# One constant to the front of GpSimd's stream, and a later start for the first filter and table loads, in a spectral-mixing and MLP kernel

## The chip, the cores and the metric

One core of one Trainium2 chip. The metric is the device time of one execution in microseconds, as a median of several executions. The record sorts executions into a fast and a slow state (slow: over 1.5% above the fastest of the same kernel). Profiles are of one execution; "us" positions in them count from the start of its span. A single execution scatters by about 1 us around the median.

## The reference, cut to what matters

```python
def _layernorm(x, axis=-1, eps=1e-5): ...

def reference(A_x, A_w_r, A_w_i, B_x, B_w1, B_b1, B_w2):
    # A: rfft2 over both axes, times a complex filter w_r + i w_i, irfft2
    # B: einsum with w1, + b1, mish, einsum with w2
    x = A_x                                     # (1, 2048, 1024) bf16
    x = x + A(_layernorm(x), A_w_r, A_w_i)
    x = x + B(_layernorm(x), B_w1, B_b1, B_w2)
    x = x + A(_layernorm(x), A_w_r, A_w_i)
    x = x + B(_layernorm(x), B_w1, B_b1, B_w2)
    return x
```

The Fourier transforms are done as matrix products. Only the first layernorm and the start of the first A are touched by the change.

## The kernel before

The kernel builds five instruction streams: PE (TensorE, the matrix products), DVE (VectorE), ACT (ScalarE), POOL (GpSimd) and SP (SyncE, which only issues transfers here). `self.op(engine, fn, reads=, writes=)` appends to an engine's stream and works out what it must wait for from the named resources; `self.dma(engine, ...)` does so for a transfer that this engine issues. An engine executes its stream in order. The opening issues these loads:

```python
    def prologue(self):
        sp = self.sp
        xt = self.x[0].rearrange("(t p) d -> p t d", p=P)
        for c in range(4):                       # x by rows: 16 row tiles, 4 quarters of 1 MB
            self.dma(sp, self.XS[:, 4*c:4*c+4, :], xt[:, 4*c:4*c+4, :], f"x{c}", writes=self.r_xs[4*c:4*c+4])
        # ... M0, IDF
        for q in range(4):                       # XR: x transposed for the first product, 32 pieces of 128 KB
            r = Res(f"xr{q}")
            for h in range(8):
                prog = self.pool if q and h % 2 else sp
                self.dma(prog, self.XR.ap[h:P:8, 32*q:32*q+32, :], xv[h][:, 32*q:32*q+32, :], f"xr{q}{prog.name}",
                         parts=[r], reads=[self.r_xs[15]] if prog is self.pool else [])
            self.r_xr.append(r)
            if q == 2:
                self.dma(sp, self.FD[:], self.con["FD"], "fd", writes=[self.r_fd])
        # ... JT
        self.op(self.pool, lambda e: e.memset(self.EPS[:], 1e-5), writes=[self.r_eps, self.r_warm])
        self.warm(ACT.Sqrt)                      # ACT: one sqrt of EPS, so that its table is loaded early
```

`reads=[self.r_xs[15]]` on a load is a gate: the load doesn't need x, it is only held back until the last rows of x are in memory. The statistics of the 16 row tiles are then split between DVE and ACT:

```python
    def first_scales(self):
        for j in range(0, 16, 4):
            n = 2 if j % 8 else 3
            for i in range(n):
                self.stats_dve(j + i)            # bn_stats, 10 tiles in all
            for i in range(n, 4):
                self.stats_act(j + i)            # Copy and Square with accumulation, 6 tiles
            self.sums_to_mv(j + n, 4 - n)        # 3 small DVE ops: ACT's sums to mean and variance
        self.root(0, 16)                         # ACT sqrt, DVE reciprocal
        # ... PE transpose of the scales
```

After that, in `s1`, DVE and ACT scale 128 copies of a small matrix M (four groups of eight ahead of their use), PE multiplies them with XR in 16 groups of eight, and DVE and ACT copy the results out of PSUM, the memory that PE writes. Groups 0 to 3 need XR's first quarter, 4 to 7 its second, and so on. The next product stage, with FD, is called s2; the first inverse product comes later in the same A. Then the filters of `load_wr` and the tables are used:

```python
    def load_wr(self, wr, g):
        # ... for the real and the imaginary part:
            self.dma(self.pool, wr.ap[:, c, :, :], rows, "l" + wr.res.name, parts=[wr.res],
                     reads=[self.r_xs[15]] if g < 2 else [])
```

## Time and profile before

| | before |
|---|---|
| time, median | 1065.87 us (3 runs) |
| PE busy | 90% of the span |
| first PE instruction | 38.9 us |
| scaling of M starts | 39.85 us |

The chain of waits, followed back from the last instruction, in order of time (start us, us, what), is read as "this is what the end of the kernel waited for". Its first pieces and the first scaling:

```profile
2.34 11.88 DMA XS<-in_A_x_dram
14.51 7.61 POOL ARENA L249 x12
22.49 1.05 ACT ARENA L440 x2
...
39.85 3.34 DVE ARENA L573 x20
```

Load of x, then twelve DMA issues of POOL, then ACT's statistics, then DVE. L249 is the line of the helper that issues a DMA, L440 ACT's statistics, L573 the scaling of M.

### The profile page before, as it was taken

How to read it: one execution, taken by the hardware profiler on the slowest of the kernel's cores; microseconds unless marked ns; L12 is line 12 of the kernel's file. 1: busy time of each engine (PE TensorE's matmuls, PEld its weight loads, DVE VectorE, ACT ScalarE, POOL GpSimd, SP SyncE). 2: the span in 40 equal slices, each digit the busy share in tenths (PEclk: the TensorE clock that was granted, in tenths of full speed). 3: DMA queues.
4: the chain of work that ended last, by engine and by line, in shares of the span. 5: the costliest groups of instructions: out<-in, count | busy, mean ns of one | idle time of the engine just before them, and what ended most of it. 6: DMA issues, size and time to landing. Idle time of an engine off the chain costs nothing.

```text
span 1065.6 us, 14183 instructions
## 1 busy us (share of the span) xinstructions
PE 959.8 (90%) x6033; PEld 513.0 (48%) x6033; DVE 352.0 (33%) x776; ACT 336.5 (32%) x503; POOL 71.0 (7%) x114
## 2 busy tenths in 40 slices
PE   0389768999999999999977985899999999999998
PEld 0267556444444444444435764754444444444443
DVE  2879755260343200023434775526011100000111
ACT  2888635333000143410006963533400014341000
POOL 4024000000000000000530200000000000000000
PEclk9999969999999999999998995999999999999999
DMA  9639860456111122000751677045611122200000
GB/s 278 159 94 310 229 170 13 151 173 207 46 55 45 44 79 60 1 10 20 191 103 23 210 202 186 1 145 191 199 45 35 54 66 73 66 1 10 21 20 30
DMA packets 152718, 107.01 MB, mean 100 GB/s; under 512 B 74288, under 2 KB 131888, under 8 KB 152656
## 3 DMA queue, kind: packets, MB, share of 16 engines
q1 hardware_dynamic: 139936, 75.99, 24.9%
q0 software_dynamic: 9632, 28.45, 9.1%
q10 hardware_dynamic: 3088, 1.67, 0.6%
q8 instruction: 48, 0.79, 0.3%
q14 instruction: 14, 0.11, 0.0%
HBM read 80.85 MB, written 20.71 MB: 95 GB/s over the span
## 4 chain that ended last, share of the span: by engine, by line
PE 79%; DVE 9%; ACT 6%; DMA 3%; issue 1%; POOL 1%; SPq 0%; ACTq 0%; DVEq 0%
PE PS L976 36%; PE PS L994 36%; PE PS L669 2%; ACT ARENA L721 2%; DVE XS L915 1%; DVE ARENA L573 1%; DMA XS<-in_A_x_dram 1%; DVE ARENA L790 1%; DVE BN L459 1%; ACT ARENA L440 1%; DMA u_scratch<-ARENA 1%; DMA ARENA<-u_scratch 1%; DVE ARENA L951 1%; DVE ARENA L596 1%; PE PS L901 1%
## 5 line engine op out<-in xcount | busy, mean ns | idle before, releaser
L976 PE MATMUL PS<-ARENA 128*128 128x512 bf16 (+1 forms) x1984 | 394.8, 361 | 8.3 <-DVE ARENA L951 7.2
L994 PE MATMUL PS<-ARENA 128*128 128x512 bf16 x1792 | 387.4, 379 | 0.0
L980 ACT ACTIVATE ARENA<-PS,B 128x512 bf16<-128x512 f32 (+1 forms) x248 | 159.8, 646 | 439.4 <-PE PS L976 439.4
L976 PEld LDWEIGHTS PS<-ARENA 128*128 128x128 bf16 x1984 | 194.4, 99 | 202.2 <-DVE ARENA L951 8.7
L994 PEld LDWEIGHTS PS<-ARENA 128*128 128x128 bf16 x1792 | 175.3, 98 | 211.4
L999 DVE TENSOR_TENSOR XS<-PS,XS 128x512 bf16<-128x512 f32 x64 | 44.3, 692 | 537.4 <-PE PS L994 537.4
L459 DVE BATCH_NORM_STATS2 BN<-XS 128x6 f32<-128x512 bf16 x104 | 67.1, 675 | 7.4 <-DMA XS<-in_A_x_dram 6.2
L915 DVE TENSOR_TENSOR XS<-PS,XS 128x512 bf16<-128x512 f32 (+1 forms) x40 | 29.1, 790 | 82.1 <-PE PS L901 82.1
L901 PE MATMUL PS<-MT,ARENA 128*128 128x32 bf16 (+1 forms) x768 | 24.7, 188 | 27.2 <-DMA ARENA<-u_scratch 24.0
L901 PEld LDWEIGHTS PS<-MT,ARENA 128*128 128x128 bf16 x768 | 23.3, 101 | 30.8 <-issue 24.3
L669 PE MATMUL PS<-FD,ARENA 128*128 128x256 bf16 (+1 forms) x256 | 34.5, 283 | 2.9 <-ACT ARENA L594 1.2
L721 ACT ACTIVATE ARENA<-PS 128x1024 bf16<-128x1024 f32 x32 | 33.8, 1058 | 8.5 <-PE PS L717 8.5
L554 PE MATMUL PS<-ARENA 128*128 128x128 f32 x1 | 0.5, 472 | 38.9 <-DVE ARENA L551 38.9
L440 ACT ACTIVATE ARENA<-XS 128x1024 bf16<-128x1024 bf16 x24 | 25.3, 1054 | 32.3 <-DVE XS L915 31.6
L750 ACT ACTIVATE ARENA<-PS 128x1024 bf16<-128x1024 f32 x32 | 33.9, 1059 | 3.7 <-PE PS L743 3.7
L249 POOL DMA_DIRECT2D xn_scratch<-ARENA x15 | 8.3, 551 | 391.1 <-DVE ARENA L498 391.1
L743 PE MATMUL PS<-ARENA 128*128 128x256 bf16 x256 | 33.2, 273 | 0.1
L431 ACT ACTIVATE RS<-MV,EPS 128x1 f32<-128x1 f32 (+1 forms) x7 | 2.0, 292 | 98.4 <-DVE MV L462 96.2
L725 DVE TENSOR_TENSOR ARENA<-ARENA 128x1024 bf16<-128x1024 bf16 x32 | 22.0, 688 | 22.7 <-ACT ARENA L721 22.7
L743 PEld LDWEIGHTS PS<-ARENA 128*128 128x128 bf16 x256 | 24.5, 98 | 10.0 <-DVE ARENA L732 1.2
L669 PEld LDWEIGHTS PS<-FD,ARENA 128*128 128x128 bf16 x256 | 25.1, 102 | 8.7 <-DVE ARENA L596 2.8
L764 PE MATMUL PS<-ARENA,BD 128*128 128x256 bf16 x192 | 25.9, 273 | 1.3 <-DVE ARENA L790 1.0
(70 smaller groups left out, 535.7 us busy)
## 6 DMA issues: line engine op xcount, KB each, us to landing
ARENA<-in_B_w_dram SPq DMA_DIRECT2D x56, 512.0 KB, 3.9
ARENA<-in_B_w_dram SPq DMA_DIRECT2D x56, 256.0 KB, 4.4
u_scratch<-ARENA SPq DMA_DIRECT2D x14, 512.0 KB, 3.4
ARENA<-u_scratch SPq DMA_DIRECT2D x14, 512.0 KB, 5.6
XS<-in_A_x_dram SPq DMA_DIRECT2D x4, 1024.0 KB, 8.7
w_scratch<-ARENA POOLq DMA_DIRECT2D x8, 512.0 KB, 5.4
ARENA<-w_scratch POOLq DMA_DIRECT2D x8, 512.0 KB, 5.1
out_dram<-XS SPq DMA_DIRECT2D x16, 256.0 KB, 2.2
```

The lines of the kernel that those rows point to most:

```text
L440: self.op(act, lambda e, i=i, f=f: e.activation(junk.ap, x, f, accum_out=sums[:, i:i + 1]), reads=[self.r_xs[j]], writes=[junk.res], parts ...
L459: self.op(self.dve, lambda e: e.bn_stats(self.BN[:, j, 6 * h:6 * h + 6], self.XS[:, j, 512 * h:512 * h + 512]), reads=[self.r_xs[j]], part ...
L669: fns.append(lambda e: e.matmul(dst, at(r), FD[:, t:t + n], start=start, stop=stop))
L721: self.op(act, lambda e: e.activation(x.ap.rearrange("p a b -> p (a b)"), ps, ACT.Copy, scale=SIG), reads=banks, writes=[x.res])
L743: fns.append(lambda e, c=c, part=part: e.matmul(ps[:, c * 256:(c + 1) * 256], yk.ap[:, part, c * P:(c + 1) * P], t[:, (128, 0)[part]:(384, ...
L750: self.op(act, lambda e: e.activation(v.ap[:, :, i, :], src, ACT.Copy), reads=banks, parts=[v.res])
L901: fns.append(lambda e, l=l: e.matmul(ps[:, w * l:w * l + w], self.UT.ap[:, u0 + l, :], self.MT[:, 8 * lo:8 * lo + w], start=True, stop=True))
L915: self.op(self.dve, lambda e: e.tensor_tensor(xs, src, xs, ALU.add), reads=rb, parts=self.r_xs[lo:lo + nb])
L976: fns.append(lambda e, db=db, bank=bank, fl=fl: e.matmul(PS[:, bank, 0:w], wb.ap[:, db, fl * P:(fl + 1) * P], x.ap[:, db, tok], start=(db ...
L980: self.op(act, lambda e, bank=bank, ft=ft: e.activation(at.ap[:, ft, tok], PS[:, bank, 0:w], ACT.Mish, bias=self.B1[:, ft:ft + 1]), reads= ...
L994: fns.append(lambda e, i=i, ft=ft: e.matmul(PS[:, bank, :], at.ap[:, ft, t * P:(t + 1) * P], W2[ft].ap[:, h * 512:(h + 1) * 512], start=(i ...
L999: self.op(dve, lambda e: e.tensor_tensor(xs, PS[:, bank, :], xs, ALU.add), reads=[self.r_bank[bank]], writes=[self.r_xs[j]])
```

## The change

Intent: let ACT's statistics start when x arrives, and keep the first filter and table loads off the DMA engines until all of XR is loaded.

```diff
     def prologue(self):
         sp = self.sp
+        self.op(self.pool, lambda e: e.memset(self.EPS[:], 1e-5), writes=[self.r_eps, self.r_warm])
+        self.warm(ACT.Sqrt)
         xt = self.x[0].rearrange("(t p) d -> p t d", p=P)
@@
         self.JT, self.r_jt = small["JT"].ap, small["JT"].res
-        self.op(self.pool, lambda e: e.memset(self.EPS[:], 1e-5), writes=[self.r_eps, self.r_warm])
-        self.warm(ACT.Sqrt)
         self.w1_next = 0
@@ def load_wr
-                     reads=[self.r_xs[15]] if g < 2 else [])
+                     reads=[self.r_xr[3]] if g < 2 else [])
```

## The prediction

> **What bounds the kernel now.** I read the page first (engine shares, chain, waits), then the timeline of the first 65 us, because both edits touch only instructions that run there, then the waits of that stretch, then the DMA view in short windows, and last the trace's landing records of single transfers. Over the whole span PE is 90% busy and carries 79% of the chain, but at the start it does nothing:
>
> ```profile
> PE PS L554 <- DVE ARENA L551: 38.9, 1, 38.9
> ACT EPS L424 <- POOL EPS L401: 20.3, 1, 20.3
> DVE MV L451 <- ACT ARENA L440: 15.5, 2, 14.2
> POOL ARENA L249 <- DMA XS<-in_A_x_dram: 14.1, 1, 14.1
> ```
>
> These are waits of the first 70 us: who waited for whom, us in total, times, longest. Read from the bottom they are one queue of dominoes. POOL (GpSimd) sits until the last rows of x land at 14.1; ACT waits 20.3 us for a constant that POOL writes; DVE waits 14.2 us for ACT's statistics; PE's first matmul comes at 38.9. The timeline shows why (start, us, what):
>
> ```profile
> 0.75 1.28 ACT L424 ACT_TABLE_LOAD   x1 [0.75 <-PEq L1168]
> ...
> 10.33 0.21 DVE L462 BATCH_NORM_AGGREGATE MV<-BN 128x2 f32<-128x12 f32 x1
> 14.51 7.61 POOL L249 DMA_DIRECT2D ARENA<-in_A_x_dram  x12 [14.06 <-DMA XS<-in_A_x_dram]
> 22.11 0.14 POOL L401 MEMSET EPS<- 128x32 f32 x1
> ...
> 22.29 0.20 ACT L424 ACTIVATE EPS<-EPS 128x1 f32<-128x1 f32 x1 [20.26 <-POOL EPS L401]
> 22.40 1.04 ACT L440 ACTIVATE ARENA<-XS 128x1024 bf16<-128x1024 bf16 x1
> ...
> 24.74 0.28 DVE L451 TENSOR_SCALAR MV<-BN 128x2 f32<-128x2 f32 x1 [14.21 <-ACT ARENA L440]
> ...
> 38.03 0.31 ACT L431 ACTIVATE RS<-MV,EPS 128x16 f32<-128x16 f32 x1 [1.39 <-DVE MV L453]
> ...
> 39.85 3.34 DVE L573 TENSOR_SCALAR ARENA<-ARENA 128x128 bf16<-128x128 bf16 x20
> ```
>
> The 0.14 us memset stands in POOL's stream behind twelve DMA issues (7.61 us) that themselves wait for x. The layernorm statistics of 16 row tiles are shared: DVE does ten (bn_stats), ACT six (two passes each). ACT starts at 22.40 though its first tile was in memory at 6.2, when DVE began.
>
> The other resource of this stretch is the DMA engines: busy at nearly 100% from 2 to 41 us. Two windows, 10-20 us and then 28-31 us, queue by queue (packets, MB, share of 16 engines):
>
> ```profile
> q1 hardware_dynamic: 5135, 2.46, 87.9%
> q0 software_dynamic: 167, 0.47, 19.6%
> ```
> ```profile
> q0 software_dynamic: 342, 1.12, 96.5%
> q1 hardware_dynamic: 154, 0.04, 5.8%
> ```
>
> q1 carries what SP issues (x by rows, then 20 of the 32 pieces of XR, the transposed view of x, in 256-byte rows); q0 carries what POOL issues (the other 12 pieces, then filter and table loads). At 28-31 us filters and tables take nearly everything and XR almost stops.
>
> **What the Trainium skill says.** "Trainium Architecture — The Big Picture", section "Inside one NeuronCore": engines have their own streams and synchronize only through semaphores. The trace agrees: one semaphore from a 0.14 us memset holds ACT for 20.3 us. "TensorE: Matmul & The Clock Gate", section "Architectural detail: the array is 16× 32×32, not 1× 128×128": ACT and DVE queues are strict FIFO, so ACT's ready statistics cannot pass its waiting warm-up. The trace agrees, nothing of ACT runs between 2.0 and 22.29. "DMA: Bandwidth & Descriptors", section "Issuing engines are not separate DMA queues": transfers of all issuers run on the same 16 engines and interleave. The windows above agree. "TensorE: Matmul & The Clock Gate", section "What's actually happening": the clock gate decides in free-running windows of 3413 ns. The recorded clock changes lie at 132.18, 145.83, 149.24, 156.07, which are multiples of 3.41 us apart; so a shift of the start is not passed on exactly to later stages.
>
> **The change, part by part.** Instruction counts do not change. On POOL one memset moves ahead of twelve DMA issues; the order on PE, DVE, ACT and SP is the same. The first four filter and first four table issues now wait for all of XR's last quarter instead of the last rows of x.
>
> Part 1, the memset. It runs at about 0.5 us; the warm-up follows the table load at about 2.1. Now ACT's six tiles follow the data. The four quarters of x land at 6.2, 9.0, 11.5, 14.2 (issue time plus time to landing). One tile on ACT costs 2 x (1.06 + 0.12 until the next pass) = 2.36 us. ACT: tile 3 from 6.2 to 8.6; tiles 6 and 7 from 9.0 to 13.7; tile 11 to 16.1; 14 and 15 to 20.8. DVE, by durations of before: three tiles 6.2 to 10.5; three small ops 0.54 to 11.1; two tiles 2.9 to 14.0; small ops 0.5 to 14.5; three tiles 4.2 to 18.7; small ops 0.55 to 19.25; two tiles 2.83 to 22.1; small ops 0.55 to 22.65. DVE never waits for ACT on this list, if narrowly (ACT 13.7 against DVE 14.0). Root, reciprocal, transpose and copy (38.03 to 39.85 before) take 1.8, so the scaling of M starts at 24.5 instead of 39.85: 15.35 us earlier. It cannot be the whole 20.3 us that ACT waited: 6.2 us of those are x still on its way, and DVE takes over as the bound.
>
> Part 2, the wait. The first product stage then starts at 24.5 and takes 22.2 us (39.85 to 62.05), bound by DVE. It needs XR quarter by quarter: the first at about 25.6, the second at 45.19 - 15.35 = 29.8, the third at 35.3, the fourth at 40.8. Before, the quarters were complete at 22.2, 33.9, 35.8 and 39.8 by the landing records. So without part 2 the second would come about 4 us late. With part 2, POOL's share of XR is still done by 28.5, and q1 has the engines to itself from about 27. My estimate: the second quarter's last three straggling pieces (29.9 to 33.9 before, all others by 27.1) come by 28; then 3.5 pieces left of the third at 0.25 MB/us (q1 alone did 0.48 MB in 14-16 us) end by 30, the FD table (0.65 MB at about 0.39) by 31.5, the fourth quarter's four pieces by 33 to 34. All three are in time, with 1.8, 5 and 7 us to spare.
>
> What the wait delays: filters and tables are issued from about 33.5, eight issues of 5.3 us (22.18 to 27.2 before), landing within 7 us: filter 0 by about 41, the last table by 46. The first user, the DVE copy at 61.92, moves to 46.6 and the first table's matmul from 67.9 to 52.5. At least 5 us to spare for the filter, so the new wait is hidden. JT and FD, which follow on q1, land earlier than before.
>
> Sum: 15.35 us (part 1) + 0 of cost (part 2, which protects about 4 us of it). Behind this stage each later one only shifts. 1065.87 - 15.4 = 1050.5 us, 1.4% less.
>
> **The rivals.** (a) The XR load takes the place of the memset: if q1 does not speed up, the second quarter lands near 34 and PE stalls 4 us: 1054.5. For it: the DMA engines are full until 41 us and 256-byte rows run at only 0.24 MB/us; against: what starved q1 was 1.8 MB of filters and tables, which are now gone. (b) The filters come too late: waiting for XR, then 5.3 us of issues, then landing; it would need them over 5 us later than I estimate. Each us more costs one: perhaps 1053-1056. Against it: little else is left on the queues by then. (c) ACT is slower or DVE waits for ACT: at most a us, as ACT has 1.3 us of slack at the end. (d) All 20.3 us come back: no, x's landing forbids it; the most that ACT's own start can give is 22.40 - 6.24 = 16.2. That is also why over 2% (21.3 us) is not within reach. (e) Nothing: if XR's arrival set the start. Against: in the trace of before no PE wait on XR is seen at all.
>
> **Range and chances.** The step of 15.35 is read from durations that vary by under 2%. Uncertain is a possible stall of 0 to 4 us on XR, and the clock windows, which may move one or two us either way over some six cold stretches; the three runs of before spread by 1.9. So 1050.5, and 8 in 10 within 1047.5 to 1054.5. Faster by over 2% (below 1044.6): 0.02. Slower by over 2%: 0.01. Within 2%: 0.97.
>
> **What would show it.** Right: POOL's memset before 1 us, ACT's first tile at 6.2, DVE without a wait over 1 us after 11 us, the scaling of M at 24 to 25, no PE wait on XR, the filter copy near 46.6, POOL's filter issues at 33-34. A PE or DVE wait on a DMA between 25 and 47 us shows (a) or (b). Wrong would be the sum if the stages after 47 us do not keep their lengths of before (78 us up to the first inverse product, 264.0 - 140.0 = 124 us after it).

## The result, and the profile after

The changed kernel took 1050.93 us (median of 4 runs, 1050.21 to 1051.88), against 1065.73 for the kernel before in the same rounds. The ratio is 0.9859, 95% interval 0.9842 to 0.9876, 15 us or 1.4% less. A ratio is the mean time of one kernel's fast runs over that of the other's of the same rounds, so it isn't quite the ratio of the medians.

The chain of waits of the changed kernel, first pieces:

```profile
0.74 5.50 DMA XS<-in_A_x_dram
6.27 1.30 DVE BN L459 x2
7.80 1.16 DVE BN L459 x2
...
20.34 1.16 DVE BN L459 x2
24.02 3.34 DVE ARENA L573 x20
```

POOL's issues and ACT's statistics are gone from it. The chain now waits only for the first quarter of x, and from 6.27 on it is nearly all DVE's own work; what is left out between 20.34 and 24.02 holds ACT's square root (0.32 us) and PE's transpose (0.49). The timeline around it (in brackets: idle before, and what ended it):

```profile
0.74 0.12 POOL L375 MEMSET EPS<- 128x32 f32 x1 [0.29 <-POOLq L1168]
...
2.04 0.20 ACT L424 ACTIVATE EPS<-EPS 128x1 f32<-128x1 f32 x1
...
6.27 1.06 ACT L440 ACTIVATE ARENA<-XS 128x1024 bf16<-128x1024 bf16 x1 [4.03 <-DMA XS<-in_A_x_dram]
...
22.20 0.31 ACT L431 ACTIVATE RS<-MV,EPS 128x16 f32<-128x16 f32 x1 [1.41 <-DVE MV L453]
...
34.65 0.73 POOL L249 DMA_DIRECT2D ARENA<-in_A_w_r_dram  x1 [12.61 <-DMA ARENA<-in_A_x_dram]
```

The constant is written at 0.74 instead of 22.11, ACT's first tile runs at 6.27 instead of 22.40, and the square root at 22.20 instead of 38.03. The last line is the new wait: POOL stands still for 12.61 us, until XR is complete, and then issues the filters at 34.65.

Where the time went, by landmarks of the two traces (us):

| | before | after | difference |
|---|---|---|---|
| scaling of M starts | 39.85 | 24.02 | -15.83 |
| first product to next stage (s2) | 21.08 | 21.10 | 0.0 |
| s2 to first inverse product | 77.94 | 76.89 | -1.05 |
| inverse product to second GEMM of B | 123.84 | 123.70 | -0.1 |
| from there to the second A's first product | 301.12 | 302.21 | +1.1 |
| first product to s2 in the second A | 11.49 | 12.25 | +0.8 |
| the rest (inverse product, B, end) | 489.16 | 488.28 | -0.9 |

The whole gain is made before the scaling starts. The other rows are of the size of the scatter between executions; the traces of the experiments show what two of them are (-1.05 and +0.8, see the last part of the experiments).

Landings of transfers, from the trace's landing records (us): XR's quarters were complete at 22.1, 33.9, 35.8, 39.8 before and at 21.4, 28.4, 30.5, 34.4 after; filter 0 at 29.9 before and 41.4 after.

### The profile page after: what moved, and what is told of

Read it like the earlier page. It is cut to its first block, busy times and chain, and to the rows that moved or that the text cites. A ratio compares the mean times of both kernels' runs of the same rounds, so it can differ in the third digit from the quotient of the medians.

```text
span 1049.6 us, 14096 instructions
## 1 busy us (share of the span) xinstructions
PE 952.5 (91%) x5944; PEld 511.7 (49%) x6033; DVE 350.8 (33%) x776; ACT 336.5 (32%) x503; POOL 71.0 (7%) x114
## 4 chain that ended last, share of the span: by engine, by line
PE 80%; DVE 9%; ACT 6%; DMA 3%; issue 1%; SPq 0%; ACTq 0%; DVEq 0%
PE PS L994 37%; PE PS L976 37%; DVE BN L459 2%; ACT ARENA L721 2%; PE PS L669 2%; DVE XS L915 1%; DVE ARENA L573 1%; DVE ARENA L790 1%; DMA u_scratch<-ARENA 1%; DMA ARENA<-u_scratch 1%; ACT ARENA L704 1%; DVE ARENA L951 1%; DVE ARENA L596 1%; PE PS L901 1%; ACT ARENA L792 1%
## 5 line engine op out<-in xcount | busy, mean ns | idle before, releaser
L976 PE MATMUL PS<-ARENA 128*128 128x512 bf16 (+1 forms) x1946 | 390.6, 360 | 10.3 <-DVE ARENA L951 7.2
L901 PE MATMUL PS<-MT,ARENA 128*128 128x32 bf16 (+1 forms) x768 | 24.5, 187 | 27.2 <-DMA ARENA<-u_scratch 23.8
L440 ACT ACTIVATE ARENA<-XS 128x1024 bf16<-128x1024 bf16 x24 | 25.3, 1055 | 36.4 <-DVE XS L915 31.5
L721 ACT ACTIVATE ARENA<-PS 128x1024 bf16<-128x1024 f32 x32 | 33.9, 1060 | 8.5 <-PE PS L717 8.5
L750 ACT ACTIVATE ARENA<-PS 128x1024 bf16<-128x1024 f32 x32 | 33.9, 1061 | 3.7 <-PE PS L743 3.7
L498 DVE TENSOR_SCALAR ARENA<-XS,MV,RS 128x1024 bf16<-128x1024 bf16 x48 | 25.0, 543 | 1.0
```

Of the source, the lines that this page charges most:

```text
L721: self.op(act, lambda e: e.activation(x.ap.rearrange("p a b -> p (a b)"), ps, ACT.Copy, scale=SIG), reads=banks, writes=[x.res])
L750: self.op(act, lambda e: e.activation(v.ap[:, :, i, :], src, ACT.Copy), reads=banks, parts=[v.res])
L901: fns.append(lambda e, l=l: e.matmul(ps[:, w * l:w * l + w], self.UT.ap[:, u0 + l, :], self.MT[:, 8 * lo:8 * lo + w], start=True, stop=True))
L976: fns.append(lambda e, db=db, bank=bank, fl=fl: e.matmul(PS[:, bank, 0:w], wb.ap[:, db, fl * P:(fl + 1) * P], x.ap[:, db, tok], start=(db ...
```

## The experiments

Kernels are compared only within the same rounds.

| run | median us | ratio to before, 95% | first product at | length of the product stage |
|---|---|---|---|---|
| r0_after_again | 1051.75 | 0.9855 (0.9842 to 0.9868) | 25.12 | 21.09 |
| e1_memset_only | 1051.05 | 0.9866 (0.9848 to 0.9884) | 25.23 | 21.09 |
| e2_wait_only | 1066.23 | 0.9992 (0.9980 to 1.0005) | 41.01 | 21.10 |
| e3_late_memset_free_warmup | 1050.59 | 0.9847 (0.9833 to 0.9860) | 25.12 | 21.09 |
| e4_memset_after_first_issue | 1060.51 | 0.9937 (0.9924 to 0.9949) | 34.03 | 21.09 |
| e5_filters_later | 1051.84 | 0.9858 (0.9845 to 0.9871) | 25.31 | 21.19 |
| e6_filters_after_second_quarter | 1050.32 | 0.9839 (0.9826 to 0.9853) | 25.32 | 21.09 |
| e7_one_conversion | 1049.73 | 0.9838 (0.9825 to 0.9852) | 24.41 | 21.11 |
| r1_after_third | 1050.53 | 0.9846 (0.9832 to 0.9861) | 25.21 | 21.12 |
| e1b_memset_only_repeat | 1051.33 | 0.9853 (0.9838 to 0.9867) | 25.43 | 21.09 |
| e7b_one_conversion_repeat | 1049.41 | 0.9837 (0.9822 to 0.9852) | 24.52 | 21.08 |
| e8_second_quarter_last | 1053.87 | 0.9875 (0.9859 to 0.9892) | 25.13 | 25.45 |

r0 to e3 ran on one chip, e4 to e7 on a second, the last four on a third. "First product" and "product stage" are read in the trace of one execution each.

**r0_after_again and r1_after_third**: no edit, the changed kernel again.

> The changed kernel once more, on the same chip as the next three. Both theories: 1050.9 us within 1 us, 14.8 us less than before. In the trace the scaling of M starts at 24.0 us. Stage lengths after that may differ by 1 to 2 us from the first trace, where the cold stretches of the tensor clock fall differently; if the landmarks of this trace repeat those of the first one exactly, that reading of the differences falls.

> The changed kernel a third time, for comparison on one chip with the next three: 1050 to 1052 us, a ratio of 0.9857 within 0.0015 to before; scaling of M at 24.0 us, 21.1 us from the first product to the next stage.

Measured: ratios 0.9855 and 0.9846. In r0 the stage after s2 took 78.05 us instead of 76.89, so the landmarks of the first trace did not repeat exactly, as expected. The three ratios of the changed kernel (with 0.9859) give the size of what can't be told apart here: about 0.001, or 1 us.

**e1_memset_only**: the memset first, the filters gated by x alone as before.

```diff
-                     reads=[self.r_xr[3]] if g < 2 else [])
+                     reads=[self.r_xs[15]] if g < 2 else [])
```

> Memset first, filters and tables wait for x alone as before. My theory: ACT and DVE as in the changed kernel (scaling at 24.0 us), but filters and tables take the DMA engines from 27 to 32 us and the second quarter of XR lands at about 34 as before, while its first matmul wants it at 29.4: a PE wait of about 4.5 us on a DMA, time 1055.4 us (1054 to 1057). The rival, that the second edit is idle and the memset does it all: 1050.9 us and no PE wait on a DMA.

Measured: 1051.05 us, the same as the changed kernel, with one of four runs at 1055.38. So the step of my theory that gave 4 us to the second edit failed. The landing records say that XR did come late: its second quarter at 30.3 and its third at 36.8, while in the changed kernel PE had started the groups that need them at 29.4 and 34.9. The timeline of this run shows why that was free (PE's product groups, DVE's copies out of PSUM and scalings):

```profile
34.00 1.72 DVE L573 TENSOR_SCALAR ARENA<-ARENA 128x128 bf16<-128x128 bf16 x10
35.62 1.22 DVE L596 CAST ARENA<-PS 128x1024 bf16<-128x1024 f32 x1
...
36.76 1.72 DVE L573 TENSOR_SCALAR ARENA<-ARENA 128x128 bf16<-128x128 bf16 x10
36.91 3.17 PE L588 MATMUL PS<-ARENA 128*128 128x128 bf16 x32 [2.72 <-DVE ARENA L596]
38.38 1.23 DVE L596 CAST ARENA<-PS 128x1024 bf16<-128x1024 f32 x1
```

PE waited 2.72 us and then did 32 matmuls in one go; DVE went on without a gap. The profile puts PE's wait down to DVE's copy, which ended at 36.84; XR's third quarter landed at 36.8, so here two releasers fall together. That it was XR is my reading, as PE had passed the same place at 34.88 in the changed kernel, with DVE at the same point of its work.

New theory: DVE is the bound of this stage, and PE leads it. Two lines of the changed kernel's timeline, group 4 on PE and its copy by DVE:

```profile
29.36 0.62 PE L588 MATMUL PS<-ARENA 128*128 128x128 bf16 x8 [0.57 <-DVE ARENA L573]
...
32.79 1.21 DVE L596 CAST ARENA<-PS 128x1024 bf16<-128x1024 f32 x1
```

PE starts the group at 29.36, and DVE copies it out at 32.79. The group took 0.62 us here, but groups done at PE's slower pace take about 1.0 (1.01 for the one at 33.09). Reckoned with 1.0, PE has 2.4 us of lead, and a late XR costs only what goes beyond a landing at 31.8.

**e1b_memset_only_repeat**: the same kernel again, for the scatter.

> The memset alone once more, because three of its four fast runs did as well as the changed kernel and one took 1055.38. My new reading: the second quarter of XR lands early or late by chance of its last pieces (30.3 in the traced run, 33.9 in the trace of before), and PE runs some 2.4 us ahead of the DVE copy that frees its banks, so that only a landing after about 31.8 costs. Then most runs lie at 1050 to 1052 and some few at 1053 to 1056; the median is within 1 us of the changed kernel. The rival, that 1055.38 was an accident that has nothing to do with the filters: all runs within 1052.5, as those of the changed kernel.

Measured: 1051.33 us, four runs from 1050.37 to 1052.68; XR's second quarter landed at 27.1 in the traced one. Eight runs without the wait have a mean of 1051.67, twelve runs with it (first result, r0, r1) 1051.02. The difference of 0.65 us comes from one run, 1055.38, and no trace was taken of that run. That its XR landed late is likely but not shown, and neither reading of this experiment is settled by it.

**e8_second_quarter_last**: the direct test of the lead. XR's quarters are issued in the order 1, 3, 4, 2, and the filters wait for the second.

```diff
-        for q in range(4):
-            r = Res(f"xr{q}")
+        # ... the four Res objects are now made before the loop
+        for k, q in enumerate((0, 2, 3, 1)):
+            r = self.r_xr[q]
@@
-                prog = self.pool if q and h % 2 else sp
+                prog = self.pool if k and h % 2 else sp
@@
-            if q == 2:
+            if k == 2:
@@ def load_wr
-                     reads=[self.r_xr[3]] if g < 2 else [])
+                     reads=[self.r_xr[1]] if g < 2 else [])
```

> The changed kernel with XR's second quarter issued last (order 1, 3, 4, 2; the filters wait for it, so they are issued as late as now): the same traffic, and the second quarter lands at 34.4 to 36.7, where the fourth did. The theory of the prediction, that every us after 29.4 costs one: 5.0 to 7.3 us more. The theory that a wait of PE costs only beyond the 2.4 us by which it leads DVE's copy (copy of the fifth group at 32.8, its eight matmuls take 1.0, so the harmless landing ends at 31.8): 2.6 to 4.9 us more, 1053.5 to 1056, and by the landing L in the trace itself, the stretch from the first product to the next stage is 21.1 + (L - 31.8). A third, that PE has more lead than that: less than 2 us more.

Measured: 1053.87 us, 3.3 more than the changed kernel on the same chip by the medians (ratios 0.9875 against 0.9846). The second quarter landed at 36.0. The timeline of this run:

```profile
31.15 1.71 DVE L572 TENSOR_SCALAR ARENA<-ARENA 128x128 bf16<-128x128 bf16 x10
36.08 4.58 PE L587 MATMUL PS<-ARENA 128*128 128x128 bf16 x48 [7.31 <-DMA ARENA<-in_A_x_dram]
37.13 1.22 DVE L595 CAST ARENA<-PS 128x1024 bf16<-128x1024 f32 x1 [4.28 <-PE PS L587]
```

PE waited 7.31 us on the DMA, but DVE waited only 4.28 us, and the stage grew by 25.45 - 21.10 = 4.35. The rule with 2.4 us of lead had said 21.1 + (36.0 - 31.8) = 25.3; the theory of the prediction, one us for each after 29.4, would have given 27.7. (The time grew by only 3.3 us in the medians; the landing is known for this one execution alone.) So the lead is shown: the wait of the engine that isn't the bound costs nothing until the bound itself waits.

**e2_wait_only**: the other edit alone, on the kernel before.

```diff
-                     reads=[self.r_xs[15]] if g < 2 else [])
+                     reads=[self.r_xr[3]] if g < 2 else [])
```

> Memset late as before, filters wait for all of XR. My theory: XR lands 4 to 6 us earlier than before (last quarter at 34 to 35 instead of 39.8) and nobody profits, because the start of the scaling is still set by ACT, at 39.85: 1065.7 us, within 1 us of before. The rival, that the traffic of filters and tables slowed the opening stage by itself: some us faster than before, 1060 to 1064.

Measured: 1066.23 us, ratio 0.9992, the same as before. XR's quarters landed at 20.9, 26.0, 30.6 and 34.5, over 5 us earlier than before for the last three, and the first product stayed at 41.01. Faster loads that nobody waits for gain nothing.

**e3_late_memset_free_warmup**: the constant late as before, but ACT's warm-up fed by DVE.

```diff
-        self.op(self.pool, lambda e: e.memset(self.EPS[:], 1e-5), writes=[self.r_eps, self.r_warm])
-        self.warm(ACT.Sqrt)
+        cell = Res("cell")
+        self.op(self.dve, lambda e: e.memset(self.RS[:, 3, 0:1], 1.0), writes=[cell])
+        self.op(self.act, lambda e: e.activation(self.RS[:, 3, 1:2], self.RS[:, 3, 0:1], ACT.Sqrt), reads=[cell])
@@ at the end of prologue
+        self.op(self.pool, lambda e: e.memset(self.EPS[:], 1e-5), writes=[self.r_eps, self.r_warm])
```

> The memset stays late in POOL's stream (at about 22.1 us) with the filters waiting for XR, but ACT's warm-up reads a cell that DVE writes at the start, so that nothing holds ACT's queue before the square root at about 22.2. My theory, that the loss came from a waiting instruction at the head of an in-order queue and not from the constant being late: ACT's first tile at 6.3 us, scaling at 24.0 to 24.3, 1050.9 us (1050 to 1052). The rival, that the constant itself has to be early: about 1065.7 us. A third outcome, a table load that is paid again before the square root: 1.3 us more, 1052.3.

Measured: 1050.59 us, as the changed kernel. Its timeline:

```profile
6.18 1.06 ACT L442 ACTIVATE ARENA<-XS 128x1024 bf16<-128x1024 bf16 x1 [3.94 <-DMA XS<-in_A_x_dram]
...
21.93 0.14 POOL L404 MEMSET EPS<- 128x32 f32 x1
22.17 0.31 ACT L433 ACTIVATE RS<-MV,EPS 128x16 f32<-128x16 f32 x1 [1.42 <-DVE MV L455]
```

The memset ran at 21.93, as late as before, and its real user at 22.17 didn't wait for it, if only by 0.1 us. (The two lines of 6 and 21 us are from two windows of the same timeline.) So the constant wasn't late. What cost 16 us was that an early, unimportant reader of it stood at the head of ACT's in-order stream.

**e4_memset_after_first_issue**: the memset behind one of POOL's twelve issues.

```diff
@@ at the head of prologue
-        self.op(self.pool, lambda e: e.memset(self.EPS[:], 1e-5), writes=[self.r_eps, self.r_warm])
-        self.warm(ACT.Sqrt)
@@ in the loop that issues XR
+                if (q, h) == (1, 1):
+                    self.op(self.pool, lambda e: e.memset(self.EPS[:], 1e-5), writes=[self.r_eps, self.r_warm])
+                    self.warm(ACT.Sqrt)
```

> The changed kernel with the memset behind the first of POOL's twelve issues, so that it waits for the last rows of x and one issue: it runs at about 15.1 us. My theory: ACT's six tiles take 14.2 us from 15.3, to 29.5; then 0.55 of small ops and 1.8 to the scaling, which starts at about 32.7 instead of 24.0, and ACT is the bound of the statistics again: 1050.9 + 8.8 = 1059.7 us (1058.5 to 1061). The rival, that the gain comes from overlap of the statistics with x's arrival being only partly needed (DVE the bound in any case): less than 5 us above the changed kernel.

Measured: 1060.51 us; by the ratios 0.9937 - 0.9859 = 0.0078 of 1067, 8.3 us, above the changed kernel. Its timeline, put together from several windows:

```profile
15.16 0.14 POOL L397 MEMSET EPS<- 128x32 f32 x1
...
15.45 1.04 ACT L441 ACTIVATE ARENA<-XS 128x1024 bf16<-128x1024 bf16 x1
...
17.79 0.17 DVE L452 TENSOR_SCALAR MV<-BN 128x2 f32<-128x2 f32 x1 [7.22 <-ACT ARENA L441]
...
22.58 0.17 DVE L452 TENSOR_SCALAR MV<-BN 128x4 f32<-128x4 f32 x1 [1.40 <-ACT ARENA L441]
...
30.53 0.12 DVE L452 TENSOR_SCALAR MV<-BN 128x4 f32<-128x4 f32 x1
...
32.90 0.74 DVE L574 TENSOR_SCALAR ARENA<-ARENA 128x128 bf16<-128x128 bf16 x4
```

ACT's start came 9.2 us later than in the changed kernel (15.45 against 6.27) and the scaling 8.9 us later. Of the 15.8 us between before and after, the eleven further issues account for 39.85 - 32.90 = 7.0 and the wait for the last rows of x, with one issue, for the other 8.9.

The size came as expected, the path only in part. The terms of the expectation add up to 31.85, not 32.7, and ACT was not the last: its tiles ended at 29.7, and DVE began its last conversion at 30.53 without waiting. What DVE lost were two waits earlier, 7.22 and 1.40 us, in which its conversion of ACT's sums stood at the head of its own in-order stream, with tiles behind it that were in memory. They add up to 8.6 of the 8.9 us.

**e5_filters_later**: the filters behind the conversion of B1, to use up the slack of the new wait.

```diff
-            self.open_tables(0)
-            self.constants()
+            self.constants()
+            self.open_tables(0)
```

> The changed kernel with filters and tables behind the conversion of B1 in POOL's stream, which waits for a tiny-row load that landed at 41.6 us: their issue moves from 34.7 to about 41.7, 7 us later. In the changed kernel filter 0 landed at 41.4 and its user comes at 46.1, 4.7 us of slack. My theory: the wait now shows, 7.0 - 4.7 = 2.3 us, somewhat less where the engines are empty by then: DVE waits 0.5 to 2.5 us on a DMA at L881, 1051.4 to 1053.4 us. The rival, that the new wait is already at its limit (no slack): 1057 to 1058. A third, that filters are never near the path: 1050.9.

Measured: 1051.84 us, no DVE wait at the filter's first use. The expected cost of 0.5 to 2.5 us didn't come. The issue moved by only 5.8 us (40.48 instead of 34.65), and with the other loads done filter 0 landed 4.6 us after its first issue instead of 6.8: at 45.1, with its user at 46.30. The time alone, 1051.84, would have fitted the expectation; the trace, which shows no wait, doesn't. So 5.8 us more of wait were free; 1.2 us of slack were left, and how much more would cost is open.

**e6_filters_after_second_quarter**: the filters gated by XR's second quarter.

```diff
-                     reads=[self.r_xr[3]] if g < 2 else [])
+                     reads=[self.r_xr[1]] if g < 2 else [])
```

> The changed kernel with the filters waiting for XR's second quarter only (about 28.4 us) instead of its fourth. My theory: only the second quarter had no slack (landed 28.4, wanted 29.4). Filters and tables now slow the third's rest and the fourth, which may land as late as 38 to 39.5, but the fourth is wanted at 40.3: no PE wait on a DMA, 1050.9 us within 1. The rival, that all quarters have to be protected: a PE wait on XR at the ninth or thirteenth product group, 1 to 4 us slower.

Measured: 1050.32 us, as the changed kernel. The filters were issued from 28.98; the fourth quarter of XR then landed at 40.8, and PE's 13th group began at 40.90 instead of 40.41, again without loss. It was later than the 38 to 39.5 that I had expected, and still inside the lead.

**e7_one_conversion and e7b_one_conversion_repeat**: a version suggested by the profile after. If DVE is the bound of the statistics, fewer small DVE operations should help.

```diff
-        for j in range(0, 16, 4): ...            # 4 calls of sums_to_mv
+        on_act = (3, 4, 7, 8, 11, 12)
+        for j in range(16):
+            (self.stats_act if j in on_act else self.stats_dve)(j)
+        # one set of the 3 small ops over all six tiles, by a strided view (tiles 3:15, two of each four)
```

> The changed kernel with ACT's six tiles chosen as 3, 4, 7, 8, 11, 12, so that DVE turns ACT's sums into mean and variance in one call at the end instead of four: three small ops instead of twelve. If DVE sets the end of the statistics, as I say: its ten tiles end at about 20.3, ACT's at 20.7, small ops to 21.3, scaling of M at about 23.1 instead of 24.0, 0.9 us less, 1050.0 us, which the timing may not resolve but the trace does. If ACT sets it (rival): the scaling starts at 24.0 or later.

> The version with one conversion once more, on the same chip as the changed kernel: scaling of M at 23.3 instead of 24.0 us and 0.7 us less in time, 0.07%, which these rounds may not separate from nothing. If its earlier ratio (0.9838) was real beyond that, it shows 1.5 us or more below the changed kernel here too.

Measured: 1049.73 and 1049.41 us. The timeline of the first:

```profile
20.62 0.19 ACT L440 ACTIVATION_READ_ACCUMULATOR ARENA<-XS 128x1 f32 x1
20.84 0.17 DVE L550 TENSOR_SCALAR MV<-BN 128x12 f32<-128x12 f32 x1 [0.51 <-ACT ARENA L440]
...
23.28 0.42 DVE L578 TENSOR_SCALAR ARENA<-ARENA 128x128 bf16<-128x128 bf16 x2
```

The scaling starts at 23.28 instead of 24.02; DVE now waits 0.51 us for ACT, so the two are balanced. The edit also gave ACT other tiles, but ACT ended them at 20.81 as against 20.79 in the changed kernel, so the gain is DVE's. On one chip the version took 1049.41 against 1050.53 us (ratios 0.9837 and 0.9846, whose intervals overlap): 1.1 us, between the 0.7 and the 1.5 of the expectation. In the trace it is 0.7 us ahead; in the timing it is the fastest of all that ran, but not separated from the changed kernel.

**What the 14 traces show beside the edits.** The stage from s2 to the first inverse product took 76.7 to 78.1 us in them, with unchanged code. It goes with one thing: how long after s2 began the tensor clock was granted in full. Seven of the 14:

| trace | full clock after s2's start | length of the stage |
|---|---|---|
| e8_second_quarter_last | 2.83 | 76.72 |
| after | 3.39 | 76.89 |
| e1_memset_only | 3.44 | 77.05 |
| e3_late_memset_free_warmup | 4.09 | 77.27 |
| before | 5.27 | 77.94 |
| r0_after_again | 5.52 | 78.05 |
| e5_filters_later | 5.74 | 78.04 |

Over all 14 the correlation is 0.99 and the slope 0.45 us per us. The windows of two traces of the same kernel show it: first the one in which the clock rose early, then r0 (window, its length, busy us and number of matmuls on PE, then the other engines, granted clock, DMA share, GB/s):

```profile
46.24:49.64 3.40, 3.40 (x17) 2.39 (x18) 2.50 (x4) 1.47 (x3) 0.07 (x1) 0.50 0.02 5
```
```profile
46.20:51.70 5.50, 5.50 (x28) 4.00 (x29) 2.50 (x4) 2.81 (x4) 1.99 (x3) 0.50 0.13 30
```

Both ran at half clock from the start of s2, one for 3.40 and one for 5.50 us. PE did 17 matmuls in the first and 28 in the second, the same pace, so in r0 the slow pace just lasted longer. This is the -1.05 us of the landmark table; the +0.8 in the second A goes with its clock in the same way (full 5.76 us after that stage's start, against 4.13 before). It is chance, not the change: the three traces of the changed kernel alone had full clock 3.39, 5.52 and 3.69 us after s2's start. The rows of +1.1 and -0.9 were not followed up; they are within what these three traces show of the same kernel (425.0 to 425.9 us from the first inverse product to the second A's first product, and 488.3 to 489.2 for the rest).

## Why the prediction was right

The prediction of 1050.5 us was met by 1050.93, and its range held. That it came within 0.4 us is partly luck: the one step that counts was half a microsecond too small, and executions scatter by about 1 us. By its own steps:

- **What bounded the opening.** Right. e3 shows it most sharply, as it leaves the constant late and frees ACT, and takes all of the gain. One thing in the prediction's wait table was not used: DVE's two waits for ACT's sums, 15.5 us together, are nearly the whole 15.83 that came back. DVE's own tiles had stood behind its first conversion of ACT's sums as ACT's tiles stood behind the warm-up.
- **Part 1, 15.35 us.** Right: 15.83 in the trace. The half microsecond is one term: I counted 0.5 to 0.55 us for each of the four sets of small DVE operations. The first three took 0.42 each (10.50 to 10.92 in the trace after; 34.23 to 34.65 in that of before, where I could have read it) and the last 0.55 up to the square root. With these the prediction's own list ends at 22.24 instead of 22.65; the square root began at 22.20.
- **DVE becomes the bound.** Right: the chain after 6.27 is DVE's, and DVE no longer waits for ACT. e7 (0.7 us from fewer DVE operations) bears it out, and so does e4, where a late ACT made DVE wait 8.6 us and the scaling came 8.9 us later.
- **XR's landings.** Right in the traced run: 28, 30, 33 to 34 predicted for the last three quarters, 28.4, 30.5 and 34.4 measured. In r0 the last one came at 36.7, later than the range, and cost nothing.
- **Part 2, "which protects about 4 us of it".** Wrong, and so was rival (a), "PE stalls 4 us: 1054.5". Without the second edit the time was the same to within 0.65 us in the mean. Two things were wrong in the step. I took the landing of 33.9 in the trace of before as fixed; without the wait it was 30.3 and 27.1 in the two traces taken. And I took each us that PE waits as a us of time, though DVE was named as the bound in the same paragraph; PE has 2.4 us of lead (e1, e8), so a landing at 33.9 would cost an estimated 33.9 - 31.8 = 2.1 us and not 4. The error had no effect on the predicted time, because the sum for the changed kernel holds no cost of part 2.
- **The new wait is hidden.** Right. Filter 0 landed at 41.4, as estimated, with its user at 46.1: 4.7 us to spare in the trace after, and 2.7 in r0, where it landed at 43.3 with its user at 46.04. "At least 5" was a little too much. One sum was wrong without effect: the eight issues of before, 22.18 to 27.2, take 5.0 us and not 5.3; they began at 34.65 here, not at 33 to 34.
- **Later stages only shift, give or take one or two us from the clock windows.** Right, with the sizes in the two tables above; what the clock does was seen in two stages, and the other small differences were not traced.

So the gain is the first edit's alone, and the second is at most an insurance: it makes XR's last quarters land up to 6 us earlier (34.4 against 40.9 in e1), which neither traced run without it needed. Whether it would have helped the execution of 1055.38 us is not shown.

## What to carry to other kernels

A wait in the trace names the instruction that waited, but in an in-order stream the loss falls on everything behind it; ask whether that instruction has to stand there (a warm-up that reads a late constant) before making its input earlier. Of several waits in a row, that of the engine which ends the stage showed the size of the gain here: DVE's 15.5 us, not ACT's 20.3. When a load's landing is compared with "when it is wanted", take the time at which the bound engine would notice, not the first engine that reads it: here 31.8 instead of 29.4. A gain of 1.4% from moving two lines was readable to half a microsecond from durations in the trace of before, as long as each engine's list was played through against the arrival of its data.

## What the Trainium skill lacked or had wrong

- "TensorE: Matmul & The Clock Gate", section "What's actually happening": it gives the free-running windows of 3413 ns, which the records here agree with (their changes lie multiples of 3.41 us apart), and a general size for the slow start, under 1% of a kernel's span, but not what a later full clock costs one stage. Here a stage starting at half clock lost 0.45 us for each us that full clock came later, 76.7 to 78.1 us over 14 traces. The page warns that clock records of a trace can't be fully trusted (section "Seeing it yourself"), but not of this: the clock view can read full before its first record. It reads 1.00 for 62.05 to 67.32 in the trace of before, where PE did 27 matmuls in 5.27 us, the half-clock pace of the windows above.
- "DMA: Bandwidth & Descriptors", section "Queues, rings and completion order": it says that each engine takes turns between queues by the packet. It doesn't say what a queue of 256-byte rows loses beside one of large packets. From 28 to 31 us of the trace of before, XR's queue moved 154 packets with 0.04 MB beside 342 packets with 1.12 MB of filters and tables; in the same window of the trace after, without these, it moved 955 packets with 0.83 MB. Whether the profile's packets are those of the page is not shown.
- "ScalarE: Activation LUTs", section "What ACT_TABLE_LOAD costs": it gives about 1283 ns for the load and 1380 ns more for a drain. The load took 1.28 us here, but the next ACT instruction began at 2.04 after a load from 0.74 to 2.02 (trace after), so no drain was seen behind it, nor ahead of the later load at 148.97 in the trace of before, where ACT's last instruction had ended at 148.95.
